# First MoE's weights in thirds, made two chunks at a time by 768-column operations; second MoE's first two blocks as a pair too

## The chip, the cores and the metric

The kernel runs on one core of a Trainium2 chip. The time is the device time of one execution in microseconds; the median over several executions counts, and less is better.

## The reference

Three layers in float32, one behind the other:

```python
# 4 batches, 8 heads, 768 tokens, 48 columns a head
for t in range(S):
    state = alpha[:, :, t, :, None] * state + einsum('bhd,bhe->bhde', k[:, :, t], v[:, :, t])
    y[:, :, t] = einsum('bhd,bhde->bhe', q[:, :, t], state)
# x: 3072 tokens x 384
xn = x / sqrt(mean(x * x, -1) + 1e-6) * rms_g
g = xn @ w_gate                                              # 384 x 1536
x = (g / (1 + exp(-g)) * (xn @ w_val)) @ w_out               # first MoE, 1536 x 384
h = maximum(maximum(x @ w1, x @ w2), x @ w3)                 # second MoE, 384 x 768 each
out = h @ w_out2                                             # 768 x 384
```

The weights come in as 64-bit floats.

## The kernel before, in words

**Numbers in two halves.** Each float32 operand is kept as a high half (a copy rounded to the type that TensorE multiplies, on ScalarE) and a low half (operand minus high half, on VectorE), names ending in `h` and `l`. A product is three matmuls: high x high, high x low, low x high. A product of 384 columns over 384 rows thus takes 9 matmuls, the unit `MM`.

**Weights** (class `Weights`, one object `w1` for the first MoE, 36 chunks of 128x384: gate, value and output weights of each of 12 column groups f; one, `w2`, for the second, 24 chunks). A chunk is loaded raw (`load`, line 360, on SP's queue), joined from its two 32-bit words to a float32 `cv_t` by three VectorE operations (`join`, lines 58, 59, 60, each reading what the one before wrote), copied to its high half by ScalarE (`high`, line 374), subtracted to its low half by VectorE (`low`, line 380) and tested for its range by two ScalarE operations (`check`, lines 389 and 392). A pair of chunks is joined together, the operations of the two chunks alternating.

**Attention** runs in 24 tiles of 128 tokens (class `Tile_`): inputs by 12 small transfers from the seventh tile on (line 562) and transposes on VectorE (line 585), or whole transfers (line 551) and transposes on TensorE (line 579) for the first; scans for the decay (line 607 and 620), masked products (`at`, line 666), state `S` (line 714), normalization (`r` on GpSimd, lines 702 and 705; `xn`, line 719) and the halves `xh`, `xl` (line 736).

**First MoE.** 96 slots, each a block of 384 tokens by one f. A slot is gate and value products (18 matmuls, line 769), Silu on ScalarE (`sg`, line 799), multiplication on VectorE (line 802), high half `hh` (ScalarE, 806), low half `hl` (VectorE, 810) and 9 second matmuls (line 816). The first two blocks go through f 0 to 5 while attention is still at work. Until the first value product, TensorE fills its waits with filler matmuls (line 776).

**Second MoE.** Blocks 0 and 1 are done plainly: 12 steps `z` with 27 product matmuls (line 769), two maxima on VectorE (line 957; the banks 77 and 78 hold what is compared), `hh` (961), `hl` (965) and 9 second matmuls (line 972). Blocks 2 to 7 go in three pairs (`sb` 1 to 3): 9 steps of 33 matmuls each (lines 1085 and following, products `X1` to `X7` of sums and differences of weight and token quarters, instead of 36) and then the second stage `W` (line 1313, 108 matmuls). These steps need sums of the weights, made once on VectorE for each of 9 (column pair, matrix): the whole weight again (line 1031, 128x768), five combinations of 128x128 (1036 to 1040), their halves (1050 for the low one) and a first sum.

**The order** of all this on each engine is written by a planner (`Order`): each piece of work has an engine, a cost, a due time and what it needs; a list scheduler fixes each engine's program order. At run time each engine works through its own list and waits for semaphores. SP issues nearly all DMAs in one list.

Of the kernel before, what the change touches and what calls it, by code (L numbers as in the profile page):

```python
# [16 lines left out]
I64 = mybir.dt.int64  # L17
# [264 lines left out]
def gla_moe_moe(ctx: ExitStack, tc: tile.TileContext, q, k, v, alpha, wg, wv, wo, g, w1, w2, w3, wo2, out):  # L282
# [10 lines left out]
    nw = sum(w.shape[0] * w.shape[1] for w in (wg, wv, wo, w1, w2, w3, wo2)) // (P * CW)  # L293
    stats = const.tile([P, len(tiles) * NSTAT + nw], F32, name="stats")
# [17 lines left out]
    junk = const.tile([P, 512], BF16, name="junk")  # L312
# [9 lines left out]
    class Weights:  # L322


        def __init__(self, tag, pool, bufs, chunks, where, due, needs):
# [4 lines left out]
            first = tag == "w1"  # L330
            for i in range(n):
                at = due(i) - 10 - (HEAD[i // 2] if first and i < 8 else 1.5)
                before = needs(i) + self.prev("load", i, 1) + self.prev("check", i, bufs)
# [3 lines left out]
            for i in range(0, n, 2):  # L337
                both = [j for j in (i, i + 1) if j < n]
                at = due(i) - (HEAD[i // 2] if first and i < 8 else 1 if first else 1.5)
                plan.add((tag, "join", i), "DVE", 1.3 * len(both), at,  # L340
                         [(tag, "load", j) for j in both] + self.prev("rest", i, 2) + self.prev("join", i, 2),
                         partial(self.join, both))
                plan.add((tag, "high", i), "ACT", 0.45 * len(both), at, [(tag, "join", i)] + self.needed(needs, both),
                         partial(self.high, both))
                plan.add((tag, "rest", i), "DVE", 0.47 * len(both), at + 0.2, [(tag, "high", i)],
                         partial(self.low, both))
                for j in both:
                    plan.add((tag, "check", j), "ACT", 1.42, at + 2, [(tag, "load", j)],
                             partial(self.check, j))
# [7 lines left out]
        def load(self, i, bufs):  # L357
            raw = self.pool().tile([P, CW], I64, name="raw", bufs=bufs)
            src, shape = self.chunks[i]
            nc.sync.dma_start(out=raw.rearrange("p (a b) -> p a b", a=shape[0]), in_=src)  # L360
            self.raws[i] = raw
# [9 lines left out]
        def high(self, both):  # L371
            for i in both:
# [3 lines left out]
        def low(self, both):  # L376
            for i in both:
# [6 lines left out]
        def check(self, i):  # L384
# [5 lines left out]
                junk[:, :CW], words(self.raws[i], CW)[1], AF.Square, scale=2.0**34, accum_out=stats[:, col:col + 1]  # L390
            )
            nc.scalar.activation(
                junk[:, :CW], junk[:, :CW], AF.Relu, scale=-(2.0**22), bias=bound, accum_out=small[:, n:n + 1]
# [27 lines left out]
    wgh = leftg.tile([P, KT, F1], F32R, name="wgh")  # L421
    wgl = leftg.tile([P, KT, F1], F32R, name="wgl")
# [331 lines left out]
    chunks1, where1 = [], []  # L754
    for f in range(NF1):
        fs = cols(f)
        for src, dh, dl in ((wg, wgh, wgl), (wv, wvh, wvl)):
            chunks1.append((src[:, fs].rearrange("(k p) f -> p k f", p=P), (KT, P)))
            where1.append((dh[:, :, fs], dl[:, :, fs]))
        chunks1.append((wo[fs, :].unsqueeze(1), (1, DM)))  # L760
        where1.append((woh[:, f:f + 1, :], wol[:, f:f + 1, :]))
    wts1 = Weights("w1", lambda: ap, 4, chunks1, lambda i: where1[i],
# [24 lines left out]
    for s, (blk, f, pi) in enumerate(slots):  # L787
        f0, f1 = passes[pi][1:]

        def gate(s=s, blk=blk, f=f):  # L790
            begun.append(s)
            products(banks[3][:, :NB], (wgh, wgl), (xh[blk], xl[blk]), cols(f))

        def val(s=s, blk=blk, f=f):
            products(banks[4][:, :NB], (wvh, wvl), (xh[blk], xl[blk]), cols(f))
# [16 lines left out]
        def second(s=s, f=f, f0=f0, f1=f1):  # L812
            for e in range(KT):
                es = slice(e * P, (e + 1) * P)
                for i, (w_, m_) in enumerate(((woh, hi_[s]), (woh, lo_[s]), (wol, hi_[s]))):
                    nc.tensor.matmul(  # L816
                        banks[e][:, :NB], w_[:, f, es], m_, start=f == f0 and i == 0, stop=f == f1 - 1 and i == 2
# [69 lines left out]
    EARLY = 4  # L887
    for f in range(NF2):
        for j in range(3):
            chunk2(j, f)  # L890
        if f == EARLY:
# [505 lines left out]
```

## Time and profile before

| | |
|---|---|
| time, median of 3 (lowest to highest) | 892.62 us (892.55 to 892.76) |
| the profiled execution's own time | 892.83 us |
| its span, first to last instruction | 891.0 us |
| TensorE (PE) busy | 871.4 us, 98% |
| VectorE (DVE) busy | 639.5 us, 72% |
| ScalarE (ACT) busy | 363.6 us, 41% |
| GpSimd (POOL) busy | 22.1 us, 2% |
| mean granted TensorE clock | 0.997 |

Shares are averages over stages with different limits. Matmul durations overlap, so the distance from start to start counts.

### The profile page before, as it was taken

Reading aid. Unit: us, or ns where it says so; the run is one execution under the profiler, and the core shown is the slowest. Engines: PE = TensorE matmul, PEld = TensorE weight load, DVE = VectorE, ACT = ScalarE, POOL = GpSimd, SP = SyncE. Lnnn points to the kernel's source line nnn. Section 1 sums busy time; section 2 is a strip of 40 time slices with the busy share of each in tenths; the row PEclk is TensorE's granted clock in tenths of the full one; section 3 lists DMA queues with packets and bytes.
Section 4 is the critical chain, followed back from the end, with each engine's and each line's share of the span. In section 5 each row is a group of like instructions: output and inputs, shape, how many; then the busy total and the mean of one; then the engine's idle time right before and its main releaser. Section 6 shows DMA issues by size and latency. Waiting matters only on the chain.

```text
span 891.0 us, 16476 instructions
## 1 busy us (share of the span) xinstructions
PE 871.4 (98%) x6446; PEld 848.2 (95%) x6446; DVE 639.5 (72%) x1321; ACT 363.6 (41%) x928; POOL 22.1 (2%) x66
## 2 busy tenths in 40 slices
PE   7999899999999999999999999999999999999996
PEld 6889898999999999999999999999999999999996
DVE  8999999997666666666665367559886874865780
ACT  4578776433223333333233267645333232224121
POOL 1000000000000000000000000000000000000000
PEclk9999999999999999999999999999999999999998
DMA  9835654353222223222221025321200011011001
GB/s 201 190 105 175 194 164 139 86 142 85 56 53 77 53 50 81 52 53 80 58 59 51 5 85 178 107 94 49 81 1 28 1 54 54 1 53 54 1 1 56
DMA packets 106244, 69.17 MB, mean 78 GB/s; under 512 B 49200, under 2 KB 103856, under 8 KB 106160
## 3 DMA queue, kind: packets, MB, share of 16 engines
q1 hardware_dynamic: 106160, 68.05, 28.0%
q8 instruction: 52, 0.85, 0.4%
q14 instruction: 32, 0.26, 0.1%
HBM read 57.41 MB, written 10.62 MB: 76 GB/s over the span
## 4 chain that ended last, share of the span: by engine, by line
PE 86%; DVE 6%; DMA 3%; ACT 2%; SPq 2%; issue 1%; DVEq 0%; ACTq 0%
PE bank L769 35%; PE bank L1085 17%; PE bank L816 15%; PE bank L1313 6%; PE bank L653 2%; PE bank L691 2%; PE bank L776 2%; PE bank L972 2%; DMA raw<-in_moe_w_out_dram 1%; PE bank L685 1%; PE bank L676 1%; PE bank L725 1%; SPq L562 1%; DVE cv_t L59 1%; SPq L551 1%
## 5 line engine op out<-in xcount | busy, mean ns | idle before, releaser
L802 DVE TENSOR_TENSOR sg<-sg,bank 128x384 f32<-128x384 f32 x96 | 53.0, 552 | 95.7 <-PE bank L769 95.1
L806 ACT ACTIVATE hh<-sg 128x384 fp32r<-128x384 f32 x96 | 50.0, 521 | 149.0 <-DVE sg L802 148.9
L769 PE MATMUL bank<-xh,wgh 128*128 128x384 f32 x288 | 100.7, 349 | 1.5 <-ACT sg L799 1.5
L816 PE MATMUL bank<-hh,woh 128*128 128x384 f32 x288 | 98.0, 340 | 0.0
L816 PE MATMUL bank<-hl,woh 128*128 128x384 f32 x288 | 96.6, 335 | 1.3 <-DVE hl L810 1.2
L769 PE MATMUL bank<-xl,wgh 128*128 128x384 f32 x288 | 96.7, 336 | 1.2 <-DVE xl L736 1.2
L769 PE MATMUL bank<-xh,wgl 128*128 128x384 f32 x288 | 96.9, 336 | 0.2 <-DVE wgl L380 0.2
L769 PE MATMUL bank<-xh,wvh 128*128 128x384 f32 x288 | 96.7, 336 | 0.0
L769 PE MATMUL bank<-xh,wvl 128*128 128x384 f32 x288 | 96.4, 335 | 0.0
L816 PE MATMUL bank<-hh,wol 128*128 128x384 f32 x288 | 96.3, 334 | 0.0
L769 PE MATMUL bank<-xl,wvh 128*128 128x384 f32 x288 | 96.2, 334 | 0.0
L810 DVE TENSOR_TENSOR hl<-sg,hh 128x384 fp32r<-128x384 f32 x96 | 53.4, 556 | 31.0 <-ACT hh L806 30.9
L799 ACT ACTIVATE sg<-bank 128x384 f32<-128x384 f32 x96 | 46.7, 486 | 38.0 <-PE bank L769 36.9
L769 PEld LDWEIGHTS bank<-xh,wgh 128*128 128x128 f32 x288 | 54.1, 188 | 3.4 <-ACT sg L799 1.8
L816 PEld LDWEIGHTS bank<-hl,woh 128*128 128x128 f32 x288 | 54.1, 188 | 2.2 <-DVE hl L810 2.2
L816 PEld LDWEIGHTS bank<-hh,woh 128*128 128x128 f32 x288 | 54.0, 188 | 1.9
L769 PEld LDWEIGHTS bank<-xl,wgh 128*128 128x128 f32 x288 | 54.2, 188 | 1.5 <-DVE xl L736 1.5
L769 PEld LDWEIGHTS bank<-xh,wgl 128*128 128x128 f32 x288 | 54.1, 188 | 0.9 <-DVE wgl L380 0.9
L769 PEld LDWEIGHTS bank<-xh,wvh 128*128 128x128 f32 x288 | 54.1, 188 | 0.5 <-DVE sg L802 0.5
L769 PEld LDWEIGHTS bank<-xl,wvh 128*128 128x128 f32 x288 | 54.1, 188 | 0.0
L769 PEld LDWEIGHTS bank<-xh,wvl 128*128 128x128 f32 x288 | 54.1, 188 | 0.0
L816 PEld LDWEIGHTS bank<-hh,wol 128*128 128x128 f32 x288 | 54.0, 188 | 0.0
(252 smaller groups left out, 2058.0 us busy)
## 6 DMA issues: line engine op xcount, KB each, us to landing
raw<-in_moe_w_out_dram SPq DMA_DIRECT2D x18, 384.0 KB, 3.6
raw<-in_moe_w_dram SPq DMA_DIRECT2D x18, 384.0 KB, 3.8
y_scr<-yo SPq DMA_DIRECT2D x30, 192.0 KB, 1.9
raw<-in_moe_w_gate_dram SPq DMA_DIRECT2D x12, 384.0 KB, 4.2
vt<-in_v_dram SPq DMA_DIRECT2D x24, 192.0 KB, 2.6
raw<-in_moe_w_val_dram SPq DMA_DIRECT2D x12, 384.0 KB, 4.6
out_dram<-yo SPq DMA_DIRECT2D x24, 192.0 KB, 1.9
in_al<-in_alpha_dram SPq DMA_DIRECT2D x36, 96.0 KB, 2.2
```

Of the source, the lines that this page charges most:

```text
L653: nc.tensor.matmul(self.sc[i][:, pr, :], self.kT[lo:hi, pr, :], self.qT[lo:hi, pr, :], start=True, stop=True)
L691: nc.tensor.matmul(self.y[tk, 2 * pr + i, :], at[i][:, pr, tk], vt[:, 2 * pr + i, :], start=not self.c, stop=True, skip_group_check=True,)
L769: nc.tensor.matmul(ps, w_[:, kt, col], m_[:, kt, :], start=i == 0, stop=i == 3 * KT - 1)
L776: nc.tensor.matmul(banks[4][:, 0:2 * P], ident.bitcast(BF16)[:, 0:P], mask.bitcast(BF16), start=True, stop=True)
L799: nc.scalar.activation(hid[s], banks[3][:, :NB], AF.Silu)
L802: nc.vector.tensor_tensor(hid[s], hid[s], banks[4][:, :NB], ALU.mult)
L806: nc.scalar.activation(hi_[s], hid[s], AF.Copy)
L810: nc.vector.tensor_tensor(lo_[s], hid.pop(s), hi_[s].bitcast(F32), ALU.subtract)
L816: nc.tensor.matmul(banks[e][:, :NB], w_[:, f, es], m_, start=f == f0 and i == 0, stop=f == f1 - 1 and i == 2)
L972: nc.tensor.matmul(banks[t][:, :DM], l_[:, tsl], r_[:, f, :], start=f == 0 and i == 0, stop=f == NF2 - 1 and i == 2)
L1085: nc.tensor.matmul(ps, l, r, start=start and i == 0, stop=i == 2, skip_group_check=True)
L1313: nc.tensor.matmul(banks[i][:, :DM], l, r[:, f, :], start=f == 0 and m_ == 0, stop=f == NF2 - 1 and m_ == 2)
```

## The change

**First MoE's weights.** `w1`'s chunks are no longer put into six big tensors (`wgh`, `wgl`, `wvh`, ...) but, in the order in which they are loaded, into three pairs of tensors of 12 chunks each, `third0h` to `third2l`. Two chunks that follow each other lie side by side in their raw buffer, in `cv_t` and in their third, so that each of the steps of a pair is one operation of 768 columns: three for the join, one for the high half, one for the low half (line 401 of the changed kernel), and a check over both. The two chunks' operations no longer alternate.

**Second MoE's first blocks.** Blocks 0 and 1 take only f 2 to 5 plainly (8 steps); their hidden values go into the stored tensors (`third2h`, `third2l`), and f 0 and 1 are done by three steps of the pair scheme, as are the blocks behind them. The second stage `W` (line 1337) then follows for all f in place of line 972. The weights of f 2 and 3 are loaded first, the output weights last.

**Sums.** They pass through one buffer `wh`: the whole weight again by GpSimd for six of nine (line 1040, for n > 2), the combinations in place (1049 to 1053), the low half (1062), and the first sums (1070 to 1072) always in the weight's own place.

Lines of the changed kernel that answer to lines of before: products 797 (769), fillers 804 (776), `mult` 830 (802), `hl` 838 (810), second matmuls 845 (816), maxima 984 (957), pair steps 1098 (1085), turn of the inputs 609 (585), twelve inputs 586 (562), raw loads 373 (360), masked products 690 (666).

```diff
         def join(self, both):
             steps = []
+            if self.wide:
+
+                t = self.pool().tile([P, 2 * CW], F32, name="cv_t", bufs=1)
+                for _ in join(nc, self.raws[both[0]], t, 2 * CW):
+                    pass
+                self.tmps[both[0]] = t
+                return
             for i in both:
...
         def low(self, both):
+            if self.wide:
+                dh, dl = self.where(both[0])
+                nc.vector.tensor_tensor(dl, self.tmps.pop(both[0]), dh.bitcast(F32), ALU.subtract)
+                return
...
-    wvh = left.tile([P, KT, F1], F32R, name="wvh")
-    wvl = left.tile([P, KT, F1], F32R, name="wvl")
-    woh = left.tile([P, NF1, DM], F32R, name="woh")
-    wol = left.tile([P, NF1, DM], F32R, name="wol")
+
+    THIRD = NF1
+    thirds = {n: [left.tile([P, THIRD, CW], F32R, name=f"third{n}{half}") for half in "hl"] for n in (1, 2)}
...
-            products(banks[3][:, :NB], (wgh, wgl), (xh[blk], xl[blk]), cols(f))
+            products(banks[3][:, :NB], w1_rows(3 * f), (xh[blk], xl[blk]), slice(0, P))
...
+    FS = 2, 3, 4, 5
+    for f in (2, 3, 0, 1, 4, 5):
...
-    NZ = PLAIN * NF2
+    NZ = PLAIN * len(FS)
...
-        plan.add(("s2", z), "PE", MM, due + 1.2, [("hl2", z), wts2.ready(index2["o", f]),
...
+        engine = nc.gpsimd if n > 2 else nc.vector
+        engine.tensor_tensor(whole[n].rearrange("p k i f -> p k (i f)"), h_, l_, ALU.add)
...
+        ready = [wts2.ready(index2[j, 2 * fp + i]) for i in range(2)] + [("sl", n - 1) if n else ("g", NS - 1)]
+        late = n > 2
+        plan.add(("sr", n), "POOL" if late else "DVE", 2.8 if late else 1.1, at - 0.5 * late, ready, partial(whole_again, n))
...
-        for step_ in range(NS1):
+        for step_ in range(LAST[sb] + 1):
```

VectorE's list where the first pair of chunks is joined, of before (lines 58 to 60 the join, each twice for two chunks; 666 the masked products; 604 the next tile's scan; 630, 719 later work of the tiles; 380 the low halves):

```order
L58 TENSOR_SCALAR cv_t<-raw 128x384 x2
L59 SCALAR_TENSOR_TENSOR cv_t<-raw,cv_t 128x384 x2
L60 SCALAR_TENSOR_TENSOR cv_t<-raw,cv_t 128x384 x2
L666 TENSOR_TENSOR at<-bank_78,mask 128x512
L666 TENSOR_TENSOR at<-bank_79,mask 128x512
L604 COPY all<-bank_80 112x4
L605 MEMSET bank_80 112x4
...
L620 SCALAR_TENSOR_TENSOR aT<-bank_80,starts 112x512
L630 TENSOR_TENSOR qT<-bank_74,aT 112x512
L719 SCALAR_TENSOR_TENSOR xn<-bank_76,r,gb 128x384
L380 TENSOR_TENSOR wgl<-cv_t,wgh 128x3x128
L380 TENSOR_TENSOR wvl<-cv_t,wvh 128x3x128
```

and of the change (lines 58 to 60 the join, 690 the masked products, 401 the low half of both chunks, 628 and on the next tile's scan):

```order
L58 TENSOR_SCALAR cv_t<-raw 128x768
L59 SCALAR_TENSOR_TENSOR cv_t<-raw,cv_t 128x768
L60 SCALAR_TENSOR_TENSOR cv_t<-raw,cv_t 128x768
L690 TENSOR_TENSOR at<-bank_78,mask 128x512
L690 TENSOR_TENSOR at<-bank_79,mask 128x512
L401 TENSOR_TENSOR third0l<-cv_t,third0h 128x768
L628 COPY all<-bank_80 112x4
L629 MEMSET bank_80 112x4
L631 SCALAR_TENSOR_TENSOR R<-bank_80,ends 112x511
L636 TENSOR_SCALAR least<-R 112x4
```

The two chunks' operations became one each, and the low half moved up to stand directly behind the masked products.

SP's list where one tile's twelve inputs stand (12 rows, of which the first and the last are shown), of before:

```order
L360 DMA raw<-in_moe_w_val_dram 128x3x128
L360 DMA raw<-in_moe_w_out_dram 128x384
L360 DMA raw<-in_moe_w_gate_dram 128x3x128
L360 DMA raw<-in_moe_w_val_dram 128x3x128
L562 DMA in_al<-in_alpha_dram 32x4x192
L562 DMA in_al<-in_alpha_dram 32x4x160
L562 DMA in_al<-in_alpha_dram 32x4x192
...
L562 DMA in_qq<-in_q_dram 32x4x160
L360 DMA raw<-in_moe_w_out_dram 128x384
L360 DMA raw<-in_moe_w_gate_dram 128x3x128
```

and of the change:

```order
L373 DMA raw<-in_moe_w_gate_dram 128x3x128
L373 DMA raw<-in_moe_w_val_dram 128x3x128
L373 DMA raw<-in_moe_w_out_dram 128x384
L586 DMA in_al<-in_alpha_dram 32x4x192
L586 DMA in_al<-in_alpha_dram 32x4x160
L586 DMA in_al<-in_alpha_dram 32x4x192
...
L586 DMA in_qq<-in_q_dram 32x4x160
L373 DMA raw<-in_moe_w_gate_dram 128x3x128
L594 DMA vt<-in_v_dram 128x8x48
```

A raw gate chunk that stood with its value chunk ahead of the inputs now stands behind the twelve.

TensorE's list where the pair steps begin, of before (1085 pair steps, 972 second matmuls of the last plain step):

```order
L1085 MATMUL bank_79<-xh,w0l 128x384
L1085 MATMUL bank_80<-raw,wvh 128x384 x2
L1085 MATMUL bank_80<-raw,wvl 128x384
L972 MATMUL bank_73<-wo2h,hh 128x384
L972 MATMUL bank_73<-wo2h,hl 128x384
L972 MATMUL bank_73<-wo2l,hh 128x384
L972 MATMUL bank_74<-wo2h,hh 128x384
...
L972 MATMUL bank_75<-wo2l,hh 128x384
L1085 MATMUL bank_76<-raw,w0h 128x384 x2
L1085 MATMUL bank_76<-raw,w0l 128x384
```

and of the change (797 the last of the plain products, 1098 pair steps):

```order
L797 MATMUL bank_78<-xl,w2h 128x384
L797 MATMUL bank_78<-xh,w2l 128x384
L1098 MATMUL bank_79<-xh,w0h 128x384
L1098 MATMUL bank_79<-xl,w0h 128x384
L1098 MATMUL bank_79<-xh,w0l 128x384
L1098 MATMUL bank_80<-raw,third1h 128x384 x2
L1098 MATMUL bank_80<-raw,third1l 128x384
L1098 MATMUL bank_76<-raw,w0h 128x384 x2
```

The second matmuls that stood among the pair's first products are gone.

VectorE's list where the fourth weight sum is made, of before (965 `hl`, 1031 the whole weight, 1036 to 1040 combinations, 957 a maximum, 1050 the low half):

```order
L1031 TENSOR_TENSOR raw<-w0h,w0l 128x768
L1036 TENSOR_TENSOR raw<-raw 128x128
L1037 TENSOR_TENSOR raw<-raw 128x128
L1038 TENSOR_TENSOR raw<-raw 128x128
L1039 TENSOR_TENSOR raw<-raw 128x128
L1040 TENSOR_TENSOR raw<-raw 128x128
L957 TENSOR_TENSOR sg<-sg,bank_77 128x384
L1050 TENSOR_TENSOR wvl<-raw,wvh 128x512
L1031 TENSOR_TENSOR raw<-w1h,w1l 128x768
```

of the change, behind the fourth sum (1051 to 1053 and 1049 combinations, 992 a low half of the hidden values, 1062 low half of the sums, 984 maxima, 1070 to 1072 and 1079 the first sum):

```order
L1053 TENSOR_TENSOR wh<-wh 128x128
L992 TENSOR_TENSOR third2l<-sg,third2h 128x384
L1062 TENSOR_TENSOR third1l<-wh,third1h 128x512
L984 TENSOR_TENSOR sg<-sg,bank_77 128x384
L1070 TENSOR_TENSOR tw<-w0h,w0l 128x128
L1071 TENSOR_TENSOR tw<-w0h,w0l 128x128
L1072 TENSOR_TENSOR tw<-tw 128x128
L984 TENSOR_TENSOR sg<-sg,bank_78 128x384
L1079 TENSOR_TENSOR w0l<-tw,w0h 128x128
L992 TENSOR_TENSOR third2l<-sg,third2h 128x384
L1049 TENSOR_TENSOR tk<-wh 128x128
```

and GpSimd's list there, of the change:

```order
L726 TENSOR_SCALAR r<-stats 128x1
L729 TENSOR_TENSOR r<-r,half 128x1
L1040 TENSOR_TENSOR wh<-w0h,w0l 128x768
L1040 TENSOR_TENSOR wh<-w1h,w1l 128x768
L1040 TENSOR_TENSOR wh<-w2h,w2l 128x768
```

The 128x768 sum has left VectorE's list and stands in GpSimd's, which before ended there with `r`.

## Rows read from the trace of the kernel before

**Rows 1.** The page's busy time, share and instructions of each engine.
```profile
PE 871.4 (98%) x6446; PEld 848.2 (95%) x6446; DVE 639.5 (72%) x1321; ACT 363.6 (41%) x928; POOL 22.1 (2%) x66
```

**Rows 2.** Windows: length, busy us (instructions) of PE, PEld, DVE, ACT, POOL, clock, DMA, GB/s.
```profile
49.00:155.00 106.00, 100.39 (x804) 95.05 (x804) 103.13 (x226) 78.57 (x217) 3.20 (x8) 1.00 0.56 163
155.00:669.00 514.00, 514.00 (x3939) 502.56 (x3938) 350.42 (x723) 201.04 (x513) 12.66 (x34) 1.00 0.25 71
```

**Rows 3.** PE's waits: us in all, times, longest.
```profile
PE bank L769 <- ACT sg L799: 1.5, 1, 1.5
...
PE bank L816 <- DVE hl L810: 1.2, 1, 1.2
...
PE bank L769 <- DVE xl L736: 1.2, 1, 1.2
```

**Rows 4.** PE's timeline at 670 us: start, duration, instruction, [idle before].
```profile
669.61 0.34 PE L1085 MATMUL bank<-raw,wvl 128*128 128x384 f32 x1
...
670.38 0.45 PE L972 MATMUL bank<-wo2h,hh 128*128 128x384 f32 x1 [0.43 <-ACT hh L961]
...
671.14 0.44 PE L972 MATMUL bank<-wo2h,hl 128*128 128x384 f32 x1 [0.32 <-DVE hl L965]
```

**Rows 5.** The chain of waits at 519 us: start, length, group.
```profile
519.24 3.12 PE bank L769 x18
```

**Rows 6.** DVE groups of 0 to 155 us: count, busy, mean ns, idle before.
```profile
L60 DVE SCALAR_TENSOR_TENSOR cv_t<-raw,cv_t 128x384 int32<-128x384 int32 x36 | 18.4, 554 | 0.0
...
L380 DVE TENSOR_TENSOR wgl<-cv_t,wgh 128x384 fp32r<-128x384 f32 x12 | 6.6, 550 | 0.0
...
L380 DVE TENSOR_TENSOR wol<-cv_t,woh 128x384 fp32r<-128x384 f32 x11 | 6.1, 553 | 0.0
...
L380 DVE TENSOR_TENSOR wvl<-cv_t,wvh 128x384 fp32r<-128x384 f32 x11 | 6.1, 551 | 0.1
```

**Rows 7.** DVE's timeline, a pair of chunks joined.
```profile
34.30 0.62 DVE L58 TENSOR_SCALAR cv_t<-raw 128x384 int32<-128x384 int32 x2
34.84 1.02 DVE L59 SCALAR_TENSOR_TENSOR cv_t<-raw,cv_t 128x384 int32<-128x384 int32 x2
35.77 1.02 DVE L60 SCALAR_TENSOR_TENSOR cv_t<-raw,cv_t 128x384 int32<-128x384 int32 x2
36.71 0.55 DVE L736 TENSOR_TENSOR xl<-bank,xh 128x384 fp32r<-128x384 f32 x1
```

**Rows 8.** DVE's timeline, sums of the second MoE's weights.
```profile
612.71 0.95 DVE L1031 TENSOR_TENSOR raw<-w0h,w0l 128x768 f32<-128x768 f32 x1
...
613.58 0.55 DVE L965 TENSOR_TENSOR hl<-sg,hh 128x384 fp32r<-128x384 f32 x1
...
614.05 0.29 DVE L1036 TENSOR_TENSOR raw<-raw 128x128 f32<-128x128 f32 x1
...
614.37 0.29 DVE L1037 TENSOR_TENSOR raw<-raw 128x128 f32<-128x128 f32 x1
...
614.58 0.29 DVE L1038 TENSOR_TENSOR raw<-raw 128x128 f32<-128x128 f32 x1
```

**Rows 9.** PE's timeline, first product and second matmul of slot 18.
```profile
49.00 0.44 PE L769 MATMUL bank<-xh,wgh 128*128 128x384 f32 x1
...
165.46 0.33 PE L816 MATMUL bank<-hh,woh 128*128 128x384 f32 x1
```

**Rows 10.** SP's timeline around twelve inputs, and the page's DMA issues.
```profile
93.48 1.76 SPq L562 DMA_DIRECT2D in_al<-in_alpha_dram  x4
...
99.13 0.38 SPq L360 DMA_DIRECT2D raw<-in_moe_w_out_dram  x1
...
raw<-in_moe_w_gate_dram SPq DMA_DIRECT2D x12, 384.0 KB, 4.2
```

**Rows 11.** POOL groups of the whole span.
```profile
L705 POOL TENSOR_TENSOR r<-r,half 128x1 f32<-128x1 f32 x24 | 13.4, 559 | 2.0
...
L444 POOL MEMSET starts<- 112x512 f32 x1 | 0.6, 602 | 0.0
```

More of the change, by code (lines that the diff above doesn't have):

```diff
@@ L329, in __init__ @@
             n = len(chunks)
-            first = tag == "w1"
+            first = self.wide = tag == "w1"
             for i in range(n):
                 at = due(i) - 10 - (HEAD[i // 2] if first and i < 8 else 1.5)
-                before = needs(i) + self.prev("load", i, 1) + self.prev("check", i, bufs)
+                before = needs(i) + self.prev("load", i, 1)
+                if not self.wide or i % 2 == 0:
+                    before += self.prev("check", i, bufs)
                 if i >= bufs:
@@ L371, in high @@
         def high(self, both):
+            if self.wide:
+                nc.scalar.activation(self.where(both[0])[0], self.tmps[both[0]], AF.Copy)
+                return
             for i in both:
@@ L957, in most, with high, low @@
             nc.vector.tensor_tensor(hid2[z], hid2[z], banks[3 + j][:, :NB], ALU.max)
[L959 to L974 removed]
+        def high(z=z, e=2 * f + blk):
+            if not stored:
+                stored.extend(left.tile([P, NF1, DM], F32R, name=nm) for nm in ("third2h", "third2l"))
+            nc.scalar.activation(stored[0][:, e, :], hid2[z], AF.Copy)
+        def low(z=z, e=2 * f + blk):
+            nc.vector.tensor_tensor(stored[1][:, e, :], hid2.pop(z), stored[0][:, e, :].bitcast(F32), ALU.subtract)
         y_in = [("yl", blk * KT + i) for i in range(KT)]
@@ L1021, in first_sum @@
         fp, j = divmod(n, 3)
-        return sums["first"][:, j, half, :] if fp == 2 else w2s[j][half][:, 0, rows_of(fp, 1)]
+        return w2s[j][half][:, 0, rows_of(fp, 1)]
     whole, five = {}, {}
@@ L1054, in first_again @@
         f1 = rows_of(fp, 1)
-        t, u = (lts[0].tile([P, NB], F32, name="hid", bufs=7)[:, 0:P] for _ in range(2))
+        both = lower().tile([P, 2, P], F32, name="tw")
+        t, u = both[:, 0], both[:, 1]
         (h0, l0), (h1, l1) = ([w_[:, k_, f1].bitcast(F32) for w_ in w2s[j]] for k_ in (0, 1))
@@ L1090, in gla_moe_moe @@
     last_pe = ("p", NZ - 1, 2)
-    for sb in range(1, NBLK // 2):
+    LAST = [2, 8, 8, 8]
+    for sb in range(NBLK // 2):
         b0, b1 = 2 * sb, 2 * sb + 1
-        at0 = NS + NZ + (sb - 1) * 11.3
+        at0 = NS + 11 + (sb - 1) * 11.3 if sb else NS + 6
         xs, T, hid3, tmp = {}, {}, {}, {}
@@ L1221, in last_add @@
                 if j == 0:
-                    hid3[fp, slot] = lts[0].tile([P, NB], F32, name="hid", bufs=7)
+                    hid3[fp, slot] = lower().tile([P, NB], F32, name="hid", bufs=6)
                 o = t if j else hid3[fp, slot]
@@ L1282, in high @@
                     if not stored:
-                        stored.extend(left.tile([P, NF1, DM], F32R, name=nm) for nm in ("woh", "wol"))
+                        stored.extend(left.tile([P, NF1, DM], F32R, name=nm) for nm in ("third2h", "third2l"))
                     nc.scalar.activation(stored[0][:, (2 * fp + i // 2) * 2 + i % 2, :], hid3[fp, i], AF.Copy)
@@ L1304, in gla_moe_moe, with second @@
             for t in range(2 * TPB):
-                def second(part=late, t=t, i=out_banks[t]):
+                def second(part=late, t=t, i=out_banks[t], order=(*FS, 0, 1) if sb == 0 else range(NF2)):
                     wo2h, wo2l = wo2s
@@ L1308, in second @@
                     tsl = slice(tt * P, (tt + 1) * P)
-                    fs = range(4, NF2) if part else range(4)
+                    fs = order[4:] if part else order[:4]
                     for f in fs:
```

232 lines of the change are left out of this document (113 added, 119 removed).

## The prediction

> **What bounds the kernel now.** I read the page's busy shares first: TensorE (PE) is busy 98% of the span of 891.0 us, so time can only come from fewer or faster PE instructions or from the 2% in which it stands idle [rows 1]. The table by stage says where that is: from 49 to 155 us PE is busy 100.39 of 106 us while VectorE (DVE) is busy 103.13; from 155 to 669 us PE is busy in every microsecond, at a granted clock of 1.00 [rows 2]. The waits name the rest: `sg`, `hl` and `xl`, all between 49 and 155 us [rows 3], and line 972 behind `hh` and `hl` at 670 us, in the change from the first MoE to the second [rows 4]. So there are three regimes. Up to about 155 us DVE's queue sets the pace, and PE's last wait there is for the `hl` of the 17th gate/value slot. Behind it only the number of matmuls counts: 18 products follow in 3.12 us, 0.1733 us each [rows 5]. After the short stall at 670 us PE is the bound again to the end.
>
> Sums are made on the profiled execution, 892.83 us = 891.0 of span and 1.8 around it; the median of the runs is 0.2 us lower, so I subtract the same differences from 892.62.
>
> **Matmuls (sure).** Blocks 0 and 1 of the second MoE took 12 x 27 products and 12 x 9 second matmuls, 432. Now 8 slots give 216 products, three pair steps 33 each, 99, and the late second stage 108: 423. Nine fewer, in a stage where PE is the bound: 9 x 0.1733 = **-1.56 us**. I see no reason that this be lost unless PE starts to wait.
>
> **First weights in wide operations.** By 155 us DVE had joined all 36 chunks of `w1` (L58, L59, L60, 36 each; L60's row stands for the three) and made 34 of the 36 low halves (L380: 12 + 11 + 11) [rows 6]. The rows' durations overlap; what counts is start to start: two L58 34.30 to 34.84, two L59 to 35.77, two L60 to 36.71 [rows 7], so 2.41 us for a pair's join, 0.27 + 0.47 + 0.47 each chunk, and a 128x384 low counts 0.47 too. Eighteen pairs' joins and 34 lows are 18 x 2.41 + 34 x 0.47 = 59.4 us.
> What a 768-wide one costs is shown by one operation of that size: L1031 starts at 612.71 and an independent operation starts at 613.58, 0.87 us later; its halves would be 0.94. But a wide join is a chain in which each operation reads what the one before it wrote, where before another chunk's operation stood between. The small sums show the price: L1036 to the L1037 that reads it 0.32 us, but 0.21 from there to the L1038 that does not need it [rows 8], so about 0.11 to 0.12 for a dependence. A wide join is then 0.47 + 0.12 (L58: twice 0.27, less the same 0.07 that L1031 saves), 0.87 + 0.12 (L59) and 0.87 (L60) = 2.45 us. Below it the bound is 2.21 (no dependence paid), above it 2.65 (a dependence paid behind L60 as well, and nothing saved by width in L58, 0.54). By 2.45 and a low of 0.87 the same point of the queue, which needs 18 joins and now 18 lows, costs 18 x 2.45 + 18 x 0.87 = 59.8 us: **+0.4, no gain**. At 2.21 it is 55.4, -3.9; at 2.65 63.4, +4.0. I take 2.45, since both parts are rows of this kernel.
> The Trainium skill (VectorE: DVE Perf Modes, section "The DRAIN you can't avoid") says that a pipeline flush follows every DVE operation and that the next operation waits for it whatever the semaphores. By that rule alone half as many operations should save half of the flushes and interleaving should be worth nothing, so it would give the 2.21 end, which is the first rival below; the start-to-start times above differ by dependence, so the trace agrees with it only in part.
> Idle time of DVE in the front: a wide join waits for both of its chunks, and the pair's first low now stands directly behind the masked products (L690), ahead of the next tile's scan, where before three other pieces of work lay between. ScalarE has a check and a copy of 768 elements to do first; I estimate 2 us of waiting there. Against it: ScalarE has one check per pair, and the first gate product stands right behind its fillers instead of behind another tile's attention products, so PE can begin somewhat before 49.00 us [rows 9]. Following both queues to the end of the 17th slot I get PE there up to 1.6 us earlier; the pure DVE sum says 0.4 later. I take the middle, **-0.6 us**.
> On SP's queue, two raw chunks (a `gate` that went ahead of a tile's twelve input transfers, for one) now stand behind them: those twelve take from 93.48 to 99.13 and the raw chunk issued behind them at 99.13 needs, as such a chunk mostly does, another 4.2 us [rows 10]. DVE has about 11 us of queue between the turn of the earlier inputs (L609), which frees their buffers, and that join; 5.6 + 4.2 and about 1 us for the turn are 10.8: nothing, or up to 2.5 us each if SP gets there late.
> Memory and stored names (thirds instead of whole weights) change no operation. PE's fillers only keep it busy before the first product.
>
> **The way into the second MoE.** Nothing of line 972 is left between the products: the hidden blocks are stored and their second matmuls come after the pair steps. Its two stalls, from 669.61 to 670.38 and on to 671.14, take 0.77 and 0.76 us where 0.17 each would do [rows 4]: **-1.2 us**. What can be late instead is `most` on bank 77 or 78, which must follow its product within two products (3.1 us), since nothing else is left for PE: 162 products in a row, 28.1 us. Between the first of the second MoE's products and the first pair step PE has 216 products and 18 matmuls of the first MoE, 40.6 us; DVE, at 0.47 for each 128x384, 0.87 for a wide sum and 0.2 to 0.3 for a 128x128 [rows 7, 8], has 31.8; I find no place where DVE is more than one product late.
> The six sums that move to GpSimd (POOL) have no row of their size. From below, a memset of 512 columns took 0.60 us and the two-input operation on one column 0.56 [rows 11]: 0.9 for 768 columns at least. From above, three such passes (two reads, one write): 2.7. I take 1.8, the middle. They form a ring through the one buffer `wh`: POOL's sum, DVE's five combines, ScalarE's high, DVE's low, the next sum. Between a low (L1062) and the next combine (L1049) DVE has two maxima, paced by PE at 1.56 us each, so a sum is hidden up to about 3 us.
> The Trainium skill (SBUF — State Buffer, section "Who interferes with whom") says that a DVE operation with two SBUF inputs and a GpSimd operation that reads SBUF exclude each other for the whole instruction. No row of before shows it, as POOL has next to nothing to do.
>
> **The sum.** -1.56 - 0.6 - 1.2 = -3.4 us: **889.3 us**, chance 0.40. Its own range is 887.5 to 891.
>
> **Rivals.**
> *Wide operations pay in full* (0.15): a join takes 2.21. DVE's queue is 4 us shorter at the 17th slot; PE's waits that can go are 1.5 + 1.2 + 1.2 us [rows 3], but slots 8 to 12 then bind, so about 3 us of it arrive: 886.2 us. For it: the 0.87 of L1031; against it: the dependent pairs.
> *The front gives back what the rest wins* (0.25): the wait for both chunks, the low that waits for ScalarE, raw chunks behind the twelve inputs, or joins of 2.6 us. Two of these at 1 to 1.5 us each instead of the -0.6 make +2.5: 892.4 us, no change. PE then waits longer at `sg` or at a third's low between 55 and 110 us.
> *POOL's sums are late* (0.12): the other side. If one takes longer than the 3 us that hide it, each of five further ones delays DVE, and PE behind it, by the excess: at 4.2 us a sum, 5 x 1.2 = 6 us, 895.3 us; it decides from about 3.7 us, where the loss equals the gain. If DVE's two-input operations were shut out for the whole of each sum it would be 6 x 1.8 = 10.8 us against the 8.8 us (40.6 - 31.8) that DVE has to spare, a loss of 2 us.
> *PE's clock falls* (0.08): the early gate is followed by a wait of some 3.6 us for the low half of a pair. Before, no wait behind 49 us was longer than 1.5 us [rows 3] and the clock stayed at 1.00 [rows 2]. Should it fall to the lower of its two levels for a few us there, a stretch of 5 us in which PE is the bound takes 5 more, of which DVE, the bound there, hides half or more: 891.5 to 894 us.
>
> **Chances.** A change under 0.2% (1.8 us) can't be told from none here. Faster: all of the forecast but a tenth, the first rival, and a little of the second (a front that only loses 1 us): 0.36 + 0.15 + 0.06 = 0.57. Same: 0.24. Slower: the POOL rival, part of the second and of the clock: 0.19. The range goes from the first rival's 886.0 to 894.0, where the POOL rival's milder half lies; it leaves out about 1 in 10 at each end.
>
> **What would show it.** In the profile after: 4,230 matmuls in the MoE lines instead of 4,239; wide L58, L59 and L60 with starts 0.59, 0.99 and 0.87 apart (0.47, 0.87, 0.87 would be the first rival); the first product before 49 us but the second matmul of slot 18 only about 0.6 us before its 165.46 [rows 9]; no PE wait between 600 and 720 us; POOL's L1040 at 1.8 us and hidden, DVE's combines with no idle time before them. I am wrong if PE waits for `third1l`, `sg` or bank 77 after 640 us, if DVE waits more than 3 us in all for raw chunks in the first 155 us, or if PE's clock in the front is not 1.00.

## The result and the profile after

The changed kernel took 898.25 us (896.33 to 898.67 in 4 runs) against 892.69 us (892.55 to 893.02 in 4) before, three of which the prediction had: ratio 1.0056, 95% interval 1.0042 to 1.007, slower by 5.6 us. The forecast was 889.3 us, the range 886.0 to 894.0. The profiled execution is the fastest of the four, 896.33 us with a span of 894.6, 3.6 us over the one of before. What follows explains these 3.6; the other runs lie 2 us higher without a trace of their own.

The page's busy time of the changed kernel, against [rows 1]:

```profile
PE 869.3 (97%) x6415; PEld 844.7 (94%) x6415; DVE 652.8 (73%) x1266; ACT 351.8 (39%) x842; POOL 36.1 (4%) x72
```

PE has 31 matmuls fewer: 22 fillers and the nine that were counted. It is busy 2.1 us less, and the span is 3.6 us longer: PE stands idle more. The windows of the changed kernel say where (columns as in [rows 2]; the last two are 5 us each):

```profile
49.00:155.00 106.00, 97.28 (x759) 91.91 (x759) 98.29 (x157) 68.11 (x147) 4.51 (x8) 0.97 0.54 160
155.00:600.00 445.00, 444.61 (x3557) 433.22 (x3556) 297.16 (x580) 174.63 (x453) 12.61 (x34) 1.00 0.29 79
60.00:65.00 5.00, 2.81 (x16) 2.12 (x16) 4.92 (x11) 3.48 (x8) 0.00 (x0) 0.84 0.79 200
65.00:70.00 5.00, 5.00 (x31) 4.29 (x29) 4.89 (x8) 2.58 (x8) 0.00 (x0) 0.50 0.32 109
```

Between 49 and 155 us VectorE (DVE), the bound there, is busy 98.29 us instead of 103.13: it waits. PE's waits in the changed kernel, against [rows 3] and [rows 4], longest first of those behind the first product:

```profile
PE bank L797 <- DVE third1l L401: 2.9, 1, 2.9
PE bank L797 <- ACT sg L827: 2.6, 3, 1.5
...
PE bank L670 <- DVE aT L644: 2.2, 1, 2.2
PE bank L1098 <- DVE hh L1239: 2.0, 1, 2.0
...
PE bank L1098 <- ACT sg L1235: 0.7, 1, 0.7
...
PE bank L797 <- DVE sg L984: 0.5, 1, 0.5
```

PE's timeline shows what that adds up to at the two points of [rows 9]:

```profile
48.76 0.44 PE L797 MATMUL bank<-xh,third0h 128*128 128x384 f32 x1
...
171.91 0.33 PE L845 MATMUL bank<-hh,third2h 128*128 128x384 f32 x1
```

The first product is 0.24 us earlier, the second matmul of slot 18 is 6.45 us later. From there on PE is busy without a break, and the delay stays: the Silu of the 90th slot, which follows PE's gate product, starts on ScalarE (ACT) at 566.20 us instead of 560.00, 6.2 us later. PE's last matmul starts at 888.63 instead of 883.77, 4.9 later. So the front loses 6.2 us and the second MoE wins 1.3. The span is only 3.6 us longer because its end, from the last matmul's start to the last instruction, took 5.9 us instead of 7.2. Between the traces of this case that end takes 5.9 to 7.9 us, and 5.9 to 7.3 between kernels with the same second MoE, so these 1.3 us are luck of the profiled execution. ACT's and PE's rows, first before, then after:

```profile
560.00 0.49 ACT L799 ACTIVATE sg<-bank 128x384 f32<-128x384 f32 x1 [0.44 <-PE bank L769]
...
883.77 0.34 PE L1313 MATMUL bank<-wo2l,woh 128*128 128x384 f32 x1
```

```profile
566.20 0.49 ACT L827 ACTIVATE sg<-bank 128x384 f32<-128x384 f32 x1 [0.45 <-PE bank L797]
...
888.63 0.34 PE L1337 MATMUL bank<-wo2l,third2h 128*128 128x384 f32 x1
```

**The front.** Up to the 17th `hl` DVE's rows give, start to start, 148.5 us of work and 4.8 of named waits before (154.10 us with what precedes), and 149.9 and 10.5 after (161.25 us). So the work grew by 1.4 us and the waits by 5.7. The operations of a wide join cost what was forecast, 0.59, 0.99 and about 0.87 us from start to start. The wide low halves cost more than the forecast 0.87: in half of the 18 the next operation starts 0.98 to 0.99 us later, and in six of these nine it is the next join, which writes the `cv_t` that the low half reads (64.75 to 65.74 below). Rows of DVE in the changed kernel:

```profile
10.79 0.56 DVE L58 TENSOR_SCALAR cv_t<-raw 128x768 int32<-128x768 int32 x1 [1.08 <-DMA raw<-in_moe_w_val_dram]
11.38 0.96 DVE L59 SCALAR_TENSOR_TENSOR cv_t<-raw,cv_t 128x768 int32<-128x768 int32 x1
12.37 0.96 DVE L60 SCALAR_TENSOR_TENSOR cv_t<-raw,cv_t 128x768 int32<-128x768 int32 x1
...
16.87 0.96 DVE L401 TENSOR_TENSOR third0l<-cv_t,third0h 128x768 fp32r<-128x768 f32 x1 [2.25 <-ACT third0h L392]
...
54.57 0.55 DVE L830 TENSOR_TENSOR sg<-sg,bank 128x384 f32<-128x384 f32 x1 [1.58 <-ACT sg L827]
...
64.75 0.95 DVE L401 TENSOR_TENSOR third0l<-cv_t,third0h 128x768 fp32r<-128x768 f32 x1
65.74 0.56 DVE L58 TENSOR_SCALAR cv_t<-raw 128x768 int32<-128x768 int32 x1
...
103.67 0.56 DVE L58 TENSOR_SCALAR cv_t<-raw 128x768 int32<-128x768 int32 x1 [0.91 <-DMA raw<-in_moe_w_gate_dram]
...
137.78 0.56 DVE L830 TENSOR_TENSOR sg<-sg,bank 128x384 f32<-128x384 f32 x1 [1.20 <-ACT third2h L392]
...
161.25 0.55 DVE L838 TENSOR_TENSOR hl<-sg,hh 128x384 fp32r<-128x384 f32 x1
```

The first wait is for the second chunk of the pair. The second is ACT's, whose rows show why: it waits for both chunks too, loads its table only then, and the high half comes behind a 768-wide check and the squares of a tile. ACT's row of before, where the table is loaded as soon as the first chunk is there, then two of the change:

```profile
7.34 1.28 ACT L389 ACT_TABLE_LOAD   x1 [7.34 <-DMA raw<-in_moe_w_gate_dram]
```

```profile
10.78 1.28 ACT L415 ACT_TABLE_LOAD   x1 [10.78 <-DMA raw<-in_moe_w_val_dram]
...
16.01 0.83 ACT L392 ACTIVATE third0h<-cv_t 128x768 fp32r<-128x768 f32 x1
```

**The second MoE.** GpSimd (POOL) took 1.95 us a sum on average (1.82 to 2.10), where the forecast took 1.8. None of VectorE's combines (L1049) waits for a sum, so in that sense they are hidden. But each of the six holds up one VectorE operation that runs beside it. DVE's rows while one runs, and once more when none does, and POOL's row:

```profile
633.61 0.55 DVE L984 TENSOR_TENSOR sg<-sg,bank 128x384 f32<-128x384 f32 x1
634.07 1.67 DVE L1070 TENSOR_TENSOR tw<-w0h,w0l 128x128 f32<-128x128 f32 x1
635.67 0.28 DVE L1071 TENSOR_TENSOR tw<-w0h,w0l 128x128 f32<-128x128 f32 x1
...
664.97 0.29 DVE L1070 TENSOR_TENSOR tw<-w0h,w0l 128x128 f32<-128x128 f32 x1
...
633.76 1.83 POOL L1040 TENSOR_TENSOR wh<-w1h,w1l 128x768 f32<-128x768 f32 x1 [9.40 <-DVE third1l L1062]
```

POOL's sum runs until 635.59. The maximum `sg` with one input in a bank takes 0.55 us as always; the first sum, with both inputs in SBUF, takes 1.67 us instead of 0.29 and ends just behind POOL's. The Trainium skill (SBUF — State Buffer, section "Who interferes with whom") says that a DVE operation with two SBUF inputs and a GpSimd operation that reads SBUF exclude each other for the whole instruction; the trace agrees, 1.4 us lost on this one.

PE's new stalls in the second MoE:

```profile
605.64 0.44 PE L797 MATMUL bank<-xh,w1h 128*128 128x384 f32 x1 [0.47 <-DVE sg L984]
...
643.82 0.62 PE L1098 MATMUL bank<-raw,third1h 128*128 128x384 f32 x2 [2.01 <-DVE hh L1239]
...
680.02 0.44 PE L1098 MATMUL bank<-xh,w0h 128*128 128x384 f32 x1 [0.68 <-ACT sg L1235]
```

From start to start, less the 0.17 us of an undisturbed matmul, they take 0.64, 2.17 and 0.84 us, 3.65 together, where the old ones of [rows 4] took 1.2.

### The profile page after: what moved, and what is told of

Its sections match the earlier page's. It is cut to its first block, busy times and chain, and to the rows that moved or that the text cites. A ratio compares the mean times of both kernels' runs of the same rounds, so it can differ in the third digit from the quotient of the medians.

```text
span 894.6 us, 16252 instructions
## 1 busy us (share of the span) xinstructions
PE 869.3 (97%) x6415; PEld 844.7 (94%) x6415; DVE 652.8 (73%) x1266; ACT 351.8 (39%) x842; POOL 36.1 (4%) x72
## 4 chain that ended last, share of the span: by engine, by line
PE 79%; DVE 14%; DMA 2%; issue 2%; ACT 2%; SPq 0%; POOL 0%; DVEq 0%; ACTq 0%; POOLq 0%
PE bank L797 30%; PE bank L1098 17%; PE bank L845 14%; PE bank L1337 6%; PE bank L677 3%; PE bank L804 2%; PE bank L715 2%; PE bank L709 1%; DVE cv_t L59 1%; PE bank L700 1%; DMA raw<-in_moe_w_gate_dram 1%; DVE cv_t L58 1%; PE bank L749 1%; PE bank L603 1%; DVE tw L1070 1%
## 5 line engine op out<-in xcount | busy, mean ns | idle before, releaser
L797 PE MATMUL bank<-xh,third0h 128*128 128x384 f32 x192 | 66.6, 347 | 1.1 <-ACT sg L827 1.1
L797 PE MATMUL bank<-xh,third1l 128*128 128x384 f32 x192 | 64.4, 335 | 2.9 <-DVE third1l L401 2.9
L797 PE MATMUL bank<-xh,third1h 128*128 128x384 f32 x192 | 65.6, 342 | 1.5 <-ACT sg L827 1.5
L797 PE MATMUL bank<-xh,third2h 128*128 128x384 f32 x192 | 65.9, 343 | 0.0
L797 PE MATMUL bank<-xh,third0l 128*128 128x384 f32 x192 | 64.8, 338 | 0.0
L797 PE MATMUL bank<-xl,third0h 128*128 128x384 f32 x192 | 64.8, 337 | 0.0
L797 PE MATMUL bank<-xh,third2l 128*128 128x384 f32 x192 | 64.4, 335 | 0.4 <-DVE third2l L401 0.4
L797 PE MATMUL bank<-xl,third1h 128*128 128x384 f32 x192 | 64.2, 335 | 0.0
L797 PE MATMUL bank<-xl,third2h 128*128 128x384 f32 x192 | 64.2, 334 | 0.0
L1337 PE MATMUL bank<-wo2l,third2h 128*128 128x384 f32 x144 | 48.1, 334 | 0.0
```

The costliest lines, as they stand in the source:

```text
L797: nc.tensor.matmul(ps, w_[:, kt, col], m_[:, kt, :], start=i == 0, stop=i == 3 * KT - 1)
L1337: nc.tensor.matmul(banks[i][:, :DM], l, r[:, f, :], start=f == order[0] and m_ == 0, stop=f == order[-1] and m_ == 2)
```

## The experiments

**The change split in four.** *e1*: the kernel before with the first half of the diff alone. *e2*: the whole change, with

```diff
-            first = self.wide = tag == "w1"
+            first = tag == "w1"
+            self.wide = False
-    junk = const.tile([P, 2 * CW], BF16, name="junk")
+    junk = const.tile([P, 512], BF16, name="junk")
```

and each chunk's third seen as 384 columns (the statistics are as long as before again, too). *e3*: the whole change with `late = False` and `engine = nc.vector`. *e4*: both of these. Expected:

> The first MoE's weights as changed (thirds, wide operations), the second MoE as before. Theory A (the front costs it: VectorE waits longer for ScalarE, raw chunks and Silu, 10.5 us against 4.8 us up to the 17th hl): about 899 us, some 6.5 us over before, and the second matmul of slot 18 at about 172 us. Theory B (the second MoE's part costs it, GpSimd's sums shutting VectorE out): about 892 to 893 us, no change against before.

> The whole change, but each weight step of the first MoE on 384 columns again, the two chunks alternating as before. Theory A: slot 18 at 165 to 166 us as before and about 891.4 us, 1.3 us under before (1.56 for nine matmuls and 1.2 for the old stall, less some 1.5 for new stalls). Theory B: about 898 us, as the whole change.

> The whole change, but all nine weight sums on VectorE. Theory A, with the second part's stalls put down to GpSimd's sums (six of 1.95 us, each holding a VectorE operation of two SBUF inputs for some 1.4 us): 2 us under the whole change, and no VectorE operation of 128x128 over 0.5 us. Rival: the sums load VectorE by 6 x 0.87 us in the stretch where it is nearly full, so TensorE waits more than before: 1 to 3 us over the whole change.

> Both at once: narrow weight steps of the first MoE and all sums on VectorE; what is left of the change is the second MoE's first blocks by the pair scheme. Theory A: about 889.9 us, 2.8 us under before. Rival (VectorE overloaded by the sums): 892 to 894 us.

Measured, beside runs of before at 893.34 us: e1 898.46 us (1.0056, 1.004 to 1.0072); e2 894.0 (1.001, 1.0 to 1.002); e3 896.95 (1.0048, 1.0032 to 1.0065); e4 893.23 (0.9998, 0.9989 to 1.0008). Theory A holds for the place: the front alone costs what the whole change costs, and with narrow operations and the order that the planner writes for them it is gone, the 17th `hl` back at 153.99 us. Its sizes for the second MoE do not hold: e2 and e4 should have won 1.3 and 2.8 us and won nothing. e3 against the whole change and e4 against e2 differ by about 1 us, within the scatter of these runs: what the sums on GpSimd cost or save in all stays unclear. In e3 and e4 no first sum is held (0.29 us each), and the stall at the first pair's first step, 2.01 us at 643.82 in the change and 1.68 at 638.17 in e2, is gone. Another came: PE waits 2.39 us in e3 and 2.36 in e4 for the first `hh` of the second pair. VectorE's list has sums in front of that `hh`, one of which waits 2.52 us for ScalarE. PE's row of e4:

```profile
675.30 0.62 PE L1099 MATMUL bank<-raw,third1h 128*128 128x384 f32 x2 [2.36 <-DVE hh L1240]
```

**The front.** *e5* is e1 with the first low half behind the next tile's scans and ScalarE's table loaded by an operation on one column at the start. *e6* is e1 with the same order and each wide operation cut in two. *e7* is e1 with other costs in the planner. *e12* is e1 with the costs of narrow operations, and each wide check in the place of the first chunk's:

```diff
# e5
+    nc.scalar.activation(junk[:, 0:1], bound, AF.Square)
-                         [(tag, "high", i)],
+                         [(tag, "high", i)] + ([("t", "br", 1)] if self.wide and i == 0 else []),
# e6
+                for h_ in (slice(0, CW), slice(CW, 2 * CW)):
+                    nc.vector.tensor_tensor(dl[:, h_], t[:, h_], dh[:, h_].bitcast(F32), ALU.subtract)
# e7
-                plan.add((tag, "join", i), "DVE", 2.25 if self.wide else 1.3 * len(both), at,
+                plan.add((tag, "join", i), "DVE", 2.6 if self.wide else 1.3 * len(both), at,
# e12
-                plan.add((tag, "join", i), "DVE", 2.25 if self.wide else 1.3 * len(both), at,
+                plan.add((tag, "join", i), "DVE", 1.3 * len(both), at,
```

(e6 cuts joins, high halves and checks in the same way; e7 also counts 2.84 for a check; e12 also 0.45 and 0.47 a chunk for the halves and the old needs of a load.)

> As the first of these (first MoE's weights as changed, second MoE as before), but the first pair's low half stands behind the next tile's scans, where it stood before, and ScalarE loads its table at the start. Theory A (waits in the front add up on VectorE): the wait of 2.3 us for ScalarE goes, the 17th hl comes 2 us or more earlier than the 162.3 us of that run, and the time is some 2 us lower, near 896.5 us. Rival (the wait is made up elsewhere, the order of the pieces sets the pace): the 17th hl at 161.5 to 162.5 us and no change.

> As the first of these, with the same order of pieces on every engine, but each piece of a pair of chunks as operations of 384 columns again (joins alternating, two high, two low, two checks). Theory A1 (the width costs: 1.4 us of VectorE work, waits for both chunks and for long ScalarE operations): the 17th hl at 157 us or earlier, the time 4 to 5 us lower than that run's 898.5. Theory A2 (the order of the pieces costs, which the planner wrote for other costs): the 17th hl at 161 to 163 us, no change.

> As the first of these, wide operations, but the planner counts 2.6 us for a join and 2.84 for a check instead of 2.25 and 2.2, which gives another order in the front. Theory A2 (the order costs): the 17th hl moves by 2 us or more either way. Theory A1 (the width costs): within 1.5 us of the 162.3 us of that run.

> First MoE's weights by wide operations, second MoE as before, the planner counting the costs of 384-column operations, with each wide check where the first chunk's check stood: a third order of the front for wide operations (the 17th hl came at 162.3 and 168.7 us in the other two, at 158.3 with the first of these orders and narrow operations, at 154.1 before). Theory A2 (the order decides more than the width): more than 3 us from 162.3. Theory A1: 160 to 164 us.

The 17th `hl` on DVE in e1, e5, e6, e7 and e12, each from its own timeline:

```profile
162.29 0.55 DVE L838 TENSOR_TENSOR hl<-sg,hh 128x384 fp32r<-128x384 f32 x1
```
```profile
159.90 0.56 DVE L839 TENSOR_TENSOR hl<-sg,hh 128x384 fp32r<-128x384 f32 x1
```
```profile
158.32 0.55 DVE L846 TENSOR_TENSOR hl<-sg,hh 128x384 fp32r<-128x384 f32 x1
```
```profile
168.69 0.55 DVE L838 TENSOR_TENSOR hl<-sg,hh 128x384 fp32r<-128x384 f32 x1
```
```profile
166.81 0.56 DVE L837 TENSOR_TENSOR hl<-sg,hh 128x384 fp32r<-128x384 f32 x1
```

The times, beside runs of before at 893.40 us (893.41 for e12): e5 896.58 us (1.0031, 1.0019 to 1.0043), e6 895.91 (1.0026, 1.0015 to 1.0036), e7 905.89 (1.0142, 1.0127 to 1.0158), e12 903.33 (1.0106, 1.009 to 1.0121). e5: its two edits together are worth 2.4 us at the 17th `hl` and 1.9 in the time, so these waits on VectorE in the front are a loss for the whole kernel and are not made up. Which of the two edits counts is open. (In e1 the wait of 2.25 us stands in two places, 1.99 us in front of the masked products and 0.26 for the high half; in e5 0.75 and none.) e6: with the order unchanged the narrow operations give back 4.0 us, nearly all of it waits (11.2 to 7.4 us of them in DVE's rows, the work 150.3 and 150.1); the time shows only 2.6 of it, and e6 has the shorter scratch tile and with it the slower pitch of the pair steps (below). The other 4.2 us to before's 154.10 are 2.6 of waits and 1.6 of work that stands in front of the 17th `hl`. They are put down to the order because nothing else is known to be left; e6 also keeps the pair's common buffers, and no run parts the two. e7 and e12: two more orders of the same wide operations come 6.4 and 4.5 us later still, about 4 us of it work that these orders put in front of the 17th `hl` (154.4 and 154.1 us against e1's 150.3). So both A1 and A2 hold, about half each for the order that the change has; neither explains the loss alone.

**The stall at the pair steps.** *e8* is e2 with the sum on GpSimd planned behind the first sum before it:

```diff
         late = n > 2
+        if late:
+            ready[-1] = ("fl", n - 1)
```

> The whole change with weight steps of 384 columns in the first MoE, and GpSimd's sums each behind the first sum's low half before them, so that no first sum meets one. Theory (a sum on GpSimd holds VectorE operations with two SBUF inputs): the first sums' operation takes 0.3 us instead of 1.7, TensorE's wait of 1.7 us at the start of the pair steps shrinks below 0.7, and the time is 1 to 2 us under the 894.0 of the narrow run, some 1 us under before. Rival (the stall is VectorE's load, not the holding): wait of 1.5 us or more and no change.

Measured 891.96 us (0.9981, 0.9972 to 0.999), faster than before by 1.4 us. But the theory behind it falls, as the rows of DVE, POOL and PE in e8 show:

```profile
634.22 0.55 DVE L1242 TENSOR_TENSOR hh<-sg,bank 128x384 f32<-128x384 f32 x1
634.68 1.47 DVE L1071 TENSOR_TENSOR tw<-w1h,w1l 128x128 f32<-128x128 f32 x1
...
633.91 2.10 POOL L1041 TENSOR_TENSOR wh<-w2h,w2l 128x768 f32<-128x768 f32 x1 [5.68 <-DVE third1l L1063]
...
633.95 0.44 PE L1101 MATMUL bank<-xh,w0h 128*128 128x384 f32 x1 [0.20 <-ACT sg L1238]
...
683.84 0.62 PE L1101 MATMUL bank<-raw,third1h 128*128 128x384 f32 x2 [0.89 <-DVE hh L1242]
```

First sums are still held, five of nine (four in the change). The planner's new condition is no wait on the chip: POOL starts as soon as its buffer is free. What changed is VectorE's order: the first pair's first `hh`, on which PE waits, now stands in front of the first sum (behind it in the change and in e2). PE's wait for it, 1.7 us in e2, is gone; 0.20 us for ScalarE is left there, and a wait of 0.89 us stands in the second pair. So that a sum is held does not by itself make PE wait; it did where `hh` stands behind it. How long that stall would be without the holding was not run with the same order.

**The pitch of the pair steps.** Comparing these traces a difference showed that no part of the change was meant to make: matmuls of the pair steps (mean of the start-to-start times between 750 and 870 us) start 0.1753 to 0.1755 us apart in before, e2, e4, e6 and e8, and 0.1733 in the changed kernel, e1, e3, e5, e7 and e12, at a clock of 1.00 in both. (The 0.1747 of the expectations below is too low; with the second stage `W`, which keeps 0.1734, the first set's mean is 0.1749 to 0.1751.) What the second set shares is a longer `junk` (768 columns instead of 512) and shorter statistics, which move all that lies behind them by 384 bytes, while `w0h` to `w2l` stay. *e9* and *e10* are the kernel before with one number changed, *e11* is e8 with it:

```diff
# e9, e11
-    junk = const.tile([P, 512], BF16, name="junk")
+    junk = const.tile([P, 704], BF16, name="junk")
# e10
-    junk = const.tile([P, 512], BF16, name="junk")
+    junk = const.tile([P, 576], BF16, name="junk")
```

> The kernel before with its scratch tile junk 384 bytes longer on each partition, which nothing uses, so that all that lies behind it on the left side of the memory (xh, xl, the first MoE's weights) moves up by 384 bytes, as in the whole change, while w0h to w2l stay. Theory P (matmuls of the pair steps start 0.1747 us apart with the old places and 0.1733 with the new ones): 0.1733 in the pair steps and 1.2 to 2 us under before. Rival (the pitch hangs on the order or on the width of what ran earlier): 0.1747 and no change.

> The same with 128 bytes. Theory P in the form that any other place will do: 0.1733 and 1 to 2 us under before. In the form that the distance between the two operands in memory counts (143,232 bytes from xh to w0h before, a multiple of 512 after 384 more are taken off): 0.174 to 0.175 and no change.

> The eighth run (second MoE's first blocks as changed, first MoE's steps on 384 columns, sums behind the first sums) with the 384 bytes. Theory P: 0.1733 in the pair steps, 1.5 us under that run's 891.96, about 890.4, 3 us under before. Rival: 892.

Measured, beside runs of before at 893.41 us: e9 890.58 us (0.9963, 0.9949 to 0.9977), e10 890.64 (0.9965, 0.9951 to 0.9978), e11 890.08 (0.9963, 0.995 to 0.9977). The window from 750 to 860 us, all of it pair steps and second stage, of before, e9 and e10:

```profile
750.00:860.00 110.00, 110.00 (x631) 110.00 (x630) 79.72 (x155) 27.39 (x57) 0.00 (x0) 1.00 0.07 22
```
```profile
750.00:860.00 110.00, 110.00 (x636) 110.00 (x636) 79.83 (x156) 27.29 (x57) 0.00 (x0) 1.00 0.07 22
```
```profile
750.00:860.00 110.00, 110.00 (x637) 110.00 (x636) 80.19 (x158) 27.26 (x57) 0.00 (x0) 1.00 0.07 22
```

PE is busy throughout in each and does 631, 636 and 637 matmuls. From the 90th Silu to the last matmul before takes 323.77 us, e9 321.74 and e10 321.84. Theory P holds: the place in memory is worth 2 us there, which is about what 891 matmuls of pair steps at 0.002 us come to. The whole of the pure padding gives 2.8 us in the median, 0.8 of which lie outside this stretch and are not explained. The form with the distance of 512 falls, since 128 bytes do as well. Which property of the place counts is open. The starts in before narrow it, for not all matmuls of these steps are slow: those of `xh` with `w0h`, `w1h` or `w2h` start 0.177 us behind the one before them, those of `xh` with `wvh` or `wvl` 0.1734; in e9 all of these start 0.173 us behind. So the place of `xh` alone does not decide it.

e11 and the two paddings of before are the fastest versions, 2.8 to 3.3 us under before; what e11 has over e9 can't be told from none.

## Why the prediction was wrong

**The matmuls.** Right: nine fewer (4,230 in the MoE lines, as forecast), 1.56 us. e2 shows it in a sum: from the 90th Silu to the last matmul it takes 324.52 us (560.30 to 884.82) against 323.77, +0.75; its new stalls (0.62, 1.84 and 0.78 us by PE's rows) are 3.2, and with -1.56 and the old stalls' -1.2 the sum comes to +0.5. For the whole change the same sum is -1.56 - 1.2 + 3.65 and some -2.0 for the pitch, -1.1; measured -1.3.

**The wide operations.** 2.45 us for a join was right (0.59 + 0.99 + 0.87; the 18 up to the 17th `hl` take 2.48 each), so the first rival is out: the chain of three pays for each dependence. The rule of the Trainium skill that the prediction set beside it (VectorE: DVE Perf Modes, section "The DRAIN you can't avoid") does not by itself tell how long three operations take; the same section says that a next operation that is not held starts earlier. The term for the low halves was too small: 18 take 16.8 us, 0.93 each, where the prediction had 0.87. With them the work grew by 1.4 us rather than 0.4. (The first rival's 886.2 us also keeps the -0.6 that its shorter queue was to replace; without it its own terms give 886.9.)

**The step that failed** is the one on idle time: "Following both queues to the end of the 17th slot I get PE there up to 1.6 us earlier; the pure DVE sum says 0.4 later. I take the middle, -0.6 us". It was +7.2 us at the 17th `hl`, 5.7 of it waits and 1.4 work. The waits that the text names were seen rightly, 2.25 us for ScalarE against an estimate of 2 and 0.91 for the raw chunk behind twelve inputs against 0 to 2.5. They were set off against an earlier first product (it came 0.24 us earlier) and fewer checks; in e5, which shortens them, the kernel is faster by nearly the whole of it, so they are not set off. And waits later in the front, for Silu behind a wide high half (1.20 us at 137.78) and behind Silu's table load (1.58 us at 54.57), were not in the sum. e6 parts them: with operations of 384 columns in the same order 3.8 us of waits go, the one behind the high half among them. A wide operation is done for both chunks at once, so that more stands behind it on ScalarE as well; that this is how the 3.8 us arise is read from the rows, not tried one by one. The wait behind the table load stays in e6, 1.60 us, and so belongs to the rest, the order that the planner wrote. Three orders of the same wide operations differ by up to 6.4 us. The second rival, the front giving back what the rest wins, was of the right kind, at +2.5 us a third of what was measured.

**The way into the second MoE.** The old stall went, as said. "I find no place where DVE is more than one product late" was wrong: 3.65 us of stalls came in its place. The longest, 2.17, stands behind a first sum held by GpSimd's, by the timeline. It is gone in e8, where `hh` stands in front of a held sum, and in e4, where no sum is held and `hh` stands in front of the first sum too; how much of it is the holding's and how much the order's is open. e4's own stall of 2.36 us, in the second pair, shows that sums put ahead of an `hh` that PE waits for, one of them waiting for ScalarE itself, are enough without any holding.

**GpSimd and the clock.** Of the POOL rival the long sums (4.2 us) did not come, 1.95 us against the forecast's 1.8; the shutting out that it names last did. It is not where the loss lies: e1 has none of it and is as slow. The clock did fall, to 0.50 in the window of 65 to 70 us, behind PE's wait of 2.2 us at 63.10 (behind the one of 2.9 us at 95.37 it stayed at 1.00). DVE was busy 4.92 and 4.89 of 5 us meanwhile, so that by this trace it cost nothing. That was only read, not tried, and other runs say that such a fall can cost. In e9's trace the clock falls there too, in before's it does not, and behind it a wait of 1.09 us appears on DVE and the 17th `hl` comes at 155.45 instead of 154.10. The windows of before and of e9, then two rows of DVE in e9:

```profile
65.00:70.00 5.00, 4.52 (x33) 3.99 (x32) 5.00 (x12) 3.70 (x12) 0.00 (x0) 1.00 0.59 177
```

```profile
65.00:70.00 5.00, 4.69 (x26) 4.27 (x27) 5.00 (x12) 2.51 (x8) 0.00 (x0) 0.66 0.70 202
```

```profile
72.62 0.56 DVE L380 TENSOR_TENSOR wvl<-cv_t,wvh 128x384 fp32r<-128x384 f32 x1 [1.09 <-ACT wvh L374]
...
155.45 0.55 DVE L810 TENSOR_TENSOR hl<-sg,hh 128x384 fp32r<-128x384 f32 x1
```

Of the 54 runs of before beside the experiments, the 12 with the lowest mean clock (0.995 and 0.996) took 894.6 us on average and the 8 with the highest (0.999) 892.9. All kernels with wide operations, and e6, had a mean clock of 0.986 to 0.995. What share of their loss is the clock's, behind PE's new waits, no run here parts.

**What was not in the sum at all** is the pitch: by e9's 2 us the change would have been slower by about 2 us more without its 384 bytes. That was worked out, not run, and these 2 us in its favour are luck.

## What to carry to other kernels

Where the queue of the engine that sets the pace is full, count the waits of a new order before the operations. Here making two pieces one saved nothing, because each operation reads the last one's output, and both chunks then waited for the later one. A dependency in this planner orders lists and does not hold an engine back on the chip; put in front what another engine waits for. Compare the start-to-start time of the same matmuls between two versions before explaining a difference: here a tile longer by 128 bytes was worth 2.8 us, where the change was to win 3.4.

## What was not expected of the hardware

Matmuls of 384 columns at a granted clock of 1.00 started 0.1753 or 0.1733 us apart in the pair steps, depending on where their operands lay: with `xh` and what lies behind it at the old place, and 128 or 384 bytes further on. That was 2 us in the stretch of these steps, and the kernel's median fell by 2.8 us of 893. A 128x128 VectorE operation with two SBUF inputs took 1.67 us beside a GpSimd sum and 0.29 without; one with an input in PSUM was not slowed.
